# Row maxima taken chunk by chunk, a three-operand sum step, a 32-byte pad and a new list order in an attention and mixture-of-experts kernel

## The chip, the cores and the metric

The kernel runs on one core of a Trainium2 chip. The metric is the device time of one execution in microseconds; lower is better. Engine names are those of the profile: PE is the matrix engine (PEld its weight loads), DVE the vector engine, ACT the scalar engine, POOL is GpSimd, and SP issues most of the DMAs.

## What is computed

Attention first: 4 batches of 8 heads, 1152 keys of 64 numbers each, and 576 pooled queries (means of two neighbours). Then a mixture of 8 experts over the 2304 rows that result, with a gate that is normalised eight times by rows and by columns. All of it is float32.

```
q_pool = q.reshape(B, H, S // 2, 2, D).mean(axis=3)
scores = q_pool @ k.T / sqrt(D);  scores -= max(scores, axis=-1)
attn = exp(scores);  attn /= attn.sum(-1) + 1e-9;  x = attn @ v
P = exp(x @ w_gate - max);  8 times: P /= P.sum(1), P /= P.sum(0), P *= N / E
out = sum over e of P[:, e] * (relu(x @ w1[e]) @ w2[e])
```

## The kernel before

Attention works on 16 pairs of heads. A pair has five units: units 0 to 3 hold 128 queries of each of the two heads, and the fifth, mixed, holds the last 64 queries of both. For each unit PE makes scores S in three chunks of 384 keys (`qk`, L460; three products of split numbers for each head, 6 matmuls a chunk, 3 in a mixed one). DVE takes each chunk and head out of PSUM into the tile E and finds its row maximum on the way (`out_max`, L468). ACT then takes the exponential of a head's 1152 keys and its row sum (`expo`, L479). S has two buffers, so PE can be two chunks ahead of DVE.

The weights must stand keys-first for the product with V. There are two ways to get there. Units 2, 3 and the mixed one go through PE (`tr`, L506) and are copied out by ACT or DVE (`tr_out`, L516 and L518); then `av` (L535) multiplies. Units 0 and 1 are turned in blocks of 32 by DVE (`turn`, L489, into the tile `turned`), and 16 DMAs from SP's queue move the blocks to their places (`front`, L547, from `turned` into `fronted`); then `av_turned` (L556) multiplies both units at once. `turned` and `fronted` have one buffer each. So the DMAs of a pair can start only when its four turns are done and `av_turned` of the pair before has read `fronted`, and the next pair's turns can start only when these DMAs have landed.

Once in a pair `rec` (L581 to L584) adds 1e-9 to nine row sums on DVE, inverts them and turns them; the result goes through DRAM (`rd`, `RB`) and POOL multiplies x by it (L604). POOL also splits the next pair's queries and keys (`q_lo`, L416, and `k_lo`, L431).

The order of attention's instructions on all engines is made by a planner (`Plan.order`, L205): each step has a cost in ns, a due time and buffers, and the planner runs a list schedule over them. The due times come from `TR0`, `TD`, `UNIT`, `MIXED` and constants in the steps. Each engine then executes its list in order.

The experts follow in 96 steps. A step makes seven products of 6 matmuls each (`product`, L745 to L747; their tile in PSUM is psh, and they stream the split tokens `xch` and `xcl`), and 36 matmuls of the second layer (L785, tile pso, streaming `w2h` and `w2l`). The right-hand end of SBUF holds `turned` and `fronted` during attention, and `xch` and `xcl` after it in the same place.

Of the kernel before, what the change touches and what calls it, by code (L numbers as in the profile page):

```python
# [5 lines left out]
F32 = mybir.dt.float32  # L6
F32R = mybir.dt.float32r
ACTF = mybir.ActivationFunctionType
ALU = mybir.AluOpType
AX = mybir.AxisListType  # L10
PSUM = bass.MemoryType.PSUM
P = 128
# [19 lines left out]
def attention_moe(tc, q, k, v, w_gate, w1, w2, out):  # L32

    nc = tc.nc  # L40
    with (
        tc.tile_pool(name="const", bufs=1) as const,
        tc.tile_pool(name="stage", bufs=1, reuse_waits="tile") as stage,
    ):
        ident = const.tile([P, P], F32, name="ident")
        x = const.tile([P, ND, N], F32, name="x")
        wg = const.tile([P, ND, 32], F32, name="wg")
        PR = const.tile([P, NT, E], F32, name="PR")

        wt = Weights(nc, stage, w1, w2)  # L50
        blocks = Blocks(nc, stage, x)

        attention(tc, q, k, v, w_gate, x, ident, wg, PR, blocks, wt)
        moe(tc, out, x, ident, wg, PR, blocks, wt)
        blocks.pool.release()
# [250 lines left out]
            o["fn"](o["on"]) if isinstance(o["eng"], tuple) else o["fn"]()  # L306


TR0 = 14.0
TD = 22.0  # L310
STICK = 4.0
GAP = 145
GAP_R = 195
CAPS = dict(kr=2, qr=2, vt=2, kT=2, qT=2, S=2, tr=3, av=1, E=4, ET=2, st=4, rs=2, rt=2, RB=2, lg=1, T=1, F=1)
UNIT, MIXED = 4.4, 3.0
PAIR = QT * UNIT + MIXED
TURNED = 2

# [1 line left out]
def cost(eng, n, psum=False, two=False):  # L320
    if eng == "ACT":
        return n / 1.2 + (55 if psum else 93)
    if eng == "DVE":
        return n / (0.96 if psum or two else 1.92) + 69
    return (n * 2.3 + 150) if two else (n * 3.45 + 100)


def attention(tc, q, k, v, w_gate, xx, ident, wg, PR, blocks, wt, dry=False, NP=NPAIRS):
# [36 lines left out]
    def op(eng, cost, prio, r=(), w=(), new=(), use=(), lat=0, mode="", after=0):  # L365
        def put(fn):
            plan.op(eng, cost, prio, fn, r, w, new, use, lat, mode, after)
        return put
# [64 lines left out]
    def unit_ops(m):  # L433
# [12 lines left out]
        for j in range(NJ):  # L446

            @op("PE", 3 * 174, T + 1.2 * j, mode="T" if mixed else "R",
                r=[("kT", p, j if first else 0), ("qT", p, min(t, 1) if first else 0)], w=[("sc", m, j)],
                new=[(("sc", m, j), "S")] + ([(("E", m), "E"), (("st", m), "st")] if j == 0 else []),  # L450
                use=[("kT", p), ("qT", p)])
            def qk(j=j):
                if j == 0:
                    D["E", m] = sbt([P, 2, S], F32, "E")
                    D["st", m] = sbt([P, 2, 4], F32, "st")
                ps = D["sc", m, j] = pst([P, 2, 512], "S")
                for i, (x, y) in enumerate(prods):
                    for h in heads:
                        rows = slice(0, P) if mixed else slice(64 * h, 64 * h + 64)
                        nc.tensor.matmul(ps[:, h, :PK], D["qT", p][rows, x, t * P:(t + 1) * P],  # L460
                                         D["kT", p][rows, y, j * PK:(j + 1) * PK], start=(i == 0), stop=(i == 2))

            for h in heads:
                @op("DVE", cost("DVE", PK, True) + 20, T + 1.2 * j + 0.7 + 0.5 * h, r=[("sc", m, j)] + [("m3", m, h, j - 1)] * (j > 0), w=[("m3", m, h, j)],
                    use=[("sc", m, j), ("E", m), ("st", m)])
                def out_max(j=j, h=h):
                    st = D["st", m]
                    nc.vector.tensor_scalar(out=D["E", m][:, h, j * PK:(j + 1) * PK], in0=D["sc", m, j][:, h, :PK], scalar1=-0.0625,  # L468
                                            scalar2=st[:, h, j - 1:j] if j else None, op0=ALU.mult, op1=ALU.min, accum_out=st[:, h, j:j + 1])

        for h in heads:
            @op("ACT", S / 1.2 + 280, T + 4.4 + 1.3 * h, r=[("m3", m, h, NJ - 1)] + ([("X", m, 0)] if h else []), w=[("X", m, h)],
                new=[(("rs", p), "rs")] if t == 0 and h == 0 else [],
                use=[("st", m), ("E", m)] + ([("rs", p)] if h or t else []))
            def expo(h=h):
                if t == 0 and h == 0:
                    D["rs", p] = sums[p % caps["rs"]]
                x = D["E", m][:, h]
                nc.scalar.activation(out=x, in_=x, func=ACTF.Exp, bias=D["st", m][:, h, NJ - 1:NJ], scale=-1.0,  # L479
                                     accum_out=D["rs", p][:, col + h * QT:col + h * QT + 1])  # L480

        if turns:
            for h in heads:
                new = t == 0 and h == 0

                @op("DVE", cost("DVE", S, two=True) + 20, T + 5.8 + 1.3 * h, r=[("X", m, h)] + ([] if new else [("Y", p, 0, 0)]), w=[("Y", p, t, h)],
                    new=[(("T", p), "T")] if new else [], use=[("E", m)] + ([] if new else [("T", p)]))
                def turn(h=h):
                    nc.vector.transpose(turned[:, :, :, h, t].rearrange("p b c j -> p c b j"), D["E", m][:, h].rearrange("p (c b j) -> p c b j", b=4, j=BK))  # L489

            return
# [46 lines left out]
        if t == QT - 1 and p < NP - 1:  # L538
            @op("SP", 1, T - UNIT * (QT - 1) + 14, r=[("Y", p, i, h) for i in range(TURNED) for h in range(2)], w=[("F", p)], new=[(("F", p), "F")], use=[("T", p)])
            def room():  # L540
                pass

            for a in range(4):
                for z in range(4):
                    @op("SP", 600, T - UNIT * (QT - 1) + 14 + 0.6 * (4 * a + z), r=[("F", p)], w=[("Z", p, a, z)], use=[("T", p), ("F", p)], lat=2500)
                    def front(a=a, z=z):
                        nc.sync.dma_start(out=fronted[BK * z:BK * z + BK, a].rearrange("p c h t j -> p (c h t j)"),  # L547
                                          in_=turned[BK * a:BK * a + BK, z].rearrange("p c h t j -> p (c h t j)"))

            for j in range(3):  # L550
                @op("PE", 6 * 2 * 53.5 * TURNED, T - UNIT * (QT - 1) + TD + 0.7 * j, mode="C", r=[("v", p)] + [("Z", p, a, z) for a in range(4) for z in range(4)],
                    w=[("av", p, mixed)], use=[("v", p), ("F", p), ("av", p, mixed)])
                def av_turned(j=j):
                    for c in range(3 * j, 3 * j + 3):
                        for h in range(2):
                            nc.tensor.matmul(D["av", p, False][64 * h:64 * h + 64, :TURNED * P], D["v", p][:, h, c, :],  # L556
                                             fronted[:, :, c, h].rearrange("p a t j -> p a (t j)"), start=(c == 0), stop=(c == NC - 1))
                    if p == NP - 2 and j == 2:
                        low.release()
                        blocks.place(tc)  # L560

        if t == QT - 1 or mixed:
            n = w if mixed else QM
            F = T + TR0 + 4.8 if mixed or p == NP - 1 else T - UNIT * (QT - 1) + TD + 3
            o = b * Q + (QM if mixed else 0)

            @op("ACT", cost("ACT", n, True) + 100, F, r=[("av", p, mixed)], w=[("xu", p, mixed)], use=[("av", p, mixed)])
            def x_out():
                y, A, i = xx[:, hp, o:o + n], D["av", p, mixed], 0
                if not mixed and p < NP - 1:  # L570
                    i = TURNED * P
                    nc.scalar.activation(out=y[:, :i].rearrange("p (t a j) -> p a t j", a=4, j=BK),
                                         in_=A[:, :i].rearrange("p (a t j) -> p a t j", a=4, j=BK), func=ACTF.Copy)
                nc.scalar.activation(out=y[:, i:], in_=A[:, i:n], func=ACTF.Copy)

        if mixed:
            @op("DVE", 400, T + 8, r=[("X", p * (QT + 1) + i, h) for i in range(QT + 1) for h in (range(2) if i < QT else (0,))],
                w=[("r", p)], new=[(("rt", p), "rt")], use=[("rs", p)])
            def rec():
                y = D["rs", p][:, :2 * QT + 1]  # L580
                nc.vector.tensor_scalar(out=y, in0=y, scalar1=1e-9, scalar2=None, op0=ALU.add)  # L581
                nc.vector.reciprocal(y, y)
                D["rt", p] = sbt([P, BK], F32, "rt")
                nc.vector.transpose(D["rt", p], D["rs", p])  # L584
# [303 lines left out]
```

## Time and profile before

| what | value |
|---|---|
| time, median of 3 runs | 1978.65 us (1976.4 to 1979.98) |
| the profiled execution's own time | 1977.72 us |
| its span | 1975.9 us |
| PE busy | 1928.4 us, 98% |
| PE weight loads busy | 1695.2 us, 86% |
| DVE busy | 1479.0 us, 75% |
| ACT busy | 836.2 us, 42% |
| POOL busy | 434.1 us, 22% |
| first matmul of the experts | at 465.50 us |

A matmul's busy time overlaps that of the next one, so a busy PE may still wait: the distance from one start to the next says more. Attention is the first 465 us; its pairs of heads repeat, so one pair can be read for fifteen.

### The profile page before, as it was taken

The numbers are of one execution on the slowest core, as the hardware profiler recorded it, in microseconds if no ns is written. First come the engines' busy times: TensorE is split into PE (matmuls) and PEld (weight loads), VectorE is DVE, ScalarE is ACT, GpSimd is POOL, SyncE is SP. The second block draws the span as 40 slices with busy tenths as digits, with TensorE's granted clock in tenths as the row PEclk, the third lists the DMA queues.
The fourth block names the chain that finished last, engine by engine and source line by source line (L and its number), as shares of the span: only waits on it lengthen the run. The fifth ranks groups of instructions, "written<-read, shape, count | busy, mean of one in ns | idle before, by whom it ended". The sixth has DMA issues, their size and how long they took to land.

```text
span 1975.9 us, 30974 instructions
## 1 busy us (share of the span) xinstructions
PE 1928.4 (98%) x11957; PEld 1695.2 (86%) x11957; DVE 1479.0 (75%) x2885; ACT 836.2 (42%) x1434; POOL 434.1 (22%) x442
## 2 busy tenths in 40 slices
PE   7999999999999999999999999999999999999999
PEld 5777777678899999999899999999989999999997
DVE  7878887888987777767867776777787677777764
ACT  5766676665433333333343333333334333333331
POOL 3222232112012121222322122221222222121210
PEclk7999999999999999999999999999999999999999
DMA  7766666532131212212222221212222122222211
GB/s 227 184 145 159 162 178 160 136 89 65 60 107 54 75 65 65 79 61 75 85 75 65 65 76 64 75 63 66 65 91 85 60 75 65 65 67 72 75 46 41
DMA packets 63221, 177.02 MB, mean 90 GB/s; under 512 B 12768, under 2 KB 22624, under 8 KB 63072
## 3 DMA queue, kind: packets, MB, share of 16 engines
q1 hardware_dynamic: 62784, 174.63, 30.2%
q8 instruction: 94, 1.54, 0.3%
q14 instruction: 55, 0.45, 0.1%
q10 hardware_dynamic: 288, 0.39, 0.1%
HBM read 134.81 MB, written 4.79 MB: 71 GB/s over the span
## 4 chain that ended last, share of the span: by engine, by line
PE 72%; DVE 3%; DMA 1%; ACT 0%; issue 0%; POOL 0%; SPq 0%; DVEq 0%; ACTq 0%
PE pso L785 37%; PE psh L747 12%; PE psh L745 12%; PE psh L746 11%; DVE w1l L147 1%; DMA w2s<-in_moe_w_dram 1%; DVE w2l L158 0%; DVE xcl L98 0%; DVE x L795 0%; DVE c L765 0%; DVE hl L755 0%; ACT w2h L157 0%; ACT hh L754 0%; POOL ca L729 0%; ACT w1h L142 0%
## 5 line engine op out<-in xcount | busy, mean ns | idle before, releaser
L745 PE MATMUL psh<-xch,w1h 128*128 128x384 f32 x1344 | 456.4, 340 | 3.1 <-ACT p L760 1.7
L746 PE MATMUL psh<-xcl,w1h 128*128 128x384 f32 x1344 | 455.5, 339 | 0.0
L747 PE MATMUL psh<-xch,w1l 128*128 128x384 f32 x1344 | 454.7, 339 | 0.7 <-DVE w1l L147 0.7
L785 PE MATMUL pso<-w2h,hh 128*128 128x512 f32 x1152 | 448.7, 389 | 0.0
L785 PE MATMUL pso<-w2l,hh 128*128 128x512 f32 x1152 | 448.7, 389 | 0.0
L785 PE MATMUL pso<-w2h,hl 128*128 128x512 f32 x1152 | 448.4, 389 | 0.0
L754 ACT ACTIVATE hh<-c 128x384 fp32r<-128x384 f32 x384 | 200.1, 522 | 289.8 <-DVE c L765 289.5
L795 DVE SCALAR_TENSOR_TENSOR x<-pso,PR,x 128x512 f32<-128x512 f32 x264 | 196.9, 746 | 152.7 <-PE pso L785 152.5
L128 POOL TENSOR_TENSOR w1t<-w1s 128x256 f32<-128x256 f32 x88 | 67.9, 771 | 1037.6 <-DMA w1s<-in_moe_w_dram 855.8
L745 PEld LDWEIGHTS psh<-xch,w1h 128*128 128x128 f32 x1344 | 252.8, 188 | 9.3 <-ACT p L760 2.4
L746 PEld LDWEIGHTS psh<-xcl,w1h 128*128 128x128 f32 x1344 | 252.7, 188 | 3.5
L785 PEld LDWEIGHTS pso<-w2h,hl 128*128 128x128 f32 x1152 | 216.2, 188 | 45.2
L747 PEld LDWEIGHTS psh<-xch,w1l 128*128 128x128 f32 x1344 | 252.6, 188 | 1.8 <-DVE w1l L147 1.6
L785 PEld LDWEIGHTS pso<-w2h,hh 128*128 128x128 f32 x1152 | 216.3, 188 | 42.1 <-ACT hh L754 0.5
L785 PEld LDWEIGHTS pso<-w2l,hh 128*128 128x128 f32 x1152 | 216.2, 188 | 41.6
L157 ACT ACTIVATE w2h<-w2s 128x1024 fp32r<-128x1024 f32 x96 | 101.9, 1061 | 274.4 <-PE pso L785 182.3
L755 DVE SCALAR_TENSOR_TENSOR hl<-c,hh 128x384 fp32r<-128x384 f32 x384 | 211.0, 550 | 3.0 <-ACT hh L754 2.2
L460 PE MATMUL S<-kT,qT 64*128 64x384 f32 (+1 forms) x1296 | 179.4, 371 | 32.4 <-DVE E L468 28.9
L479 ACT ACTIVATE E<-E,st 128x1152 f32<-128x1152 f32 x144 | 179.8, 1250 | 69.0 <-DVE E L468 68.9
L468 DVE TENSOR_SCALAR_CACHE_REDUCE E<-S,st 128x384 f32<-128x384 f32 x288 | 163.9, 606 | 50.3 <-PE S L460 48.5
L158 DVE TENSOR_TENSOR w2l<-w2s,w2h 128x1024 fp32r<-128x1024 f32 x96 | 133.3, 1388 | 84.6 <-ACT w2h L157 84.6
L760 ACT ACTIVATE p<-psh 128x384 f32<-128x384 f32 x96 | 47.1, 490 | 332.9 <-PE psh L747 332.5
(90 smaller groups left out, 2268.4 us busy)
## 6 DMA issues: line engine op xcount, KB each, us to landing
w1s<-in_moe_w_dram SPq DMA_DIRECT2D x96, 512.0 KB
w2s<-in_moe_w_dram SPq DMA_DIRECT2D x96, 512.0 KB
fronted<-turned SPq DMA_DIRECT2D x240, 144.0 KB
qr<-in_q_dram SPq DMA_DIRECT2D x15, 640.0 KB
vt<-in_v_dram SPq DMA_DIRECT2D x16, 576.0 KB
kr<-in_k_dram SPq DMA_DIRECT2D x15, 576.0 KB
out_dram<-x SPq DMA_DIRECT2D x18, 256.0 KB
RB<-rd SPq DMA_DIRECT2D x32, 128.0 KB
```

Source lines behind the costliest of these rows:

```text
L157: self.nc.scalar.activation(out=hi, in_=self.raw2[k], func=ACTF.Copy)
L158: self.nc.vector.tensor_tensor(out=lo, in0=self.raw2[k], in1=hi.bitcast(F32), op=ALU.subtract)
L460: nc.tensor.matmul(ps[:, h, :PK], D["qT", p][rows, x, t * P:(t + 1) * P], D["kT", p][rows, y, j * PK:(j + 1) * PK], start=(i == 0), stop=( ...
L468: nc.vector.tensor_scalar(out=D["E", m][:, h, j * PK:(j + 1) * PK], in0=D["sc", m, j][:, h, :PK], scalar1=-0.0625, scalar2=st[:, h, j - 1: ...
L479: nc.scalar.activation(out=x, in_=x, func=ACTF.Exp, bias=D["st", m][:, h, NJ - 1:NJ], scale=-1.0, accum_out=D["rs", p][:, col + h * QT:col ...
L745: nc.tensor.matmul(ps, hi[:, a, c, :], blocks.xch[:, b, c, :], start=(c == 0), stop=False)
L746: nc.tensor.matmul(ps, hi[:, a, c, :], blocks.xcl[:, b, c, :], start=False, stop=False)
L747: nc.tensor.matmul(ps, lo[:, a, c, :], blocks.xch[:, b, c, :], start=False, stop=(c == 1))
L754: nc.scalar.activation(out=hh[:, fh, ts], in_=src, func=ACTF.Relu)
L755: nc.vector.scalar_tensor_tensor(out=hl[:, fh, ts], in0=src, scalar=0.0, in1=hh[:, fh, ts].bitcast(F32), op0=ALU.max, op1=ALU.subtract)
L785: nc.tensor.matmul(ps, u[:, fh, ms], w[:, fh, :], start=(n == 0), stop=(n == 11))
L795: nc.vector.scalar_tensor_tensor(out=a, in0=ps, scalar=PR[:, m, e:e + 1], in1=a, op0=ALU.mult, op1=ALU.add)
```

## The change

Five things are changed.

1. `out_max` no longer passes a chunk's maximum on as the starting value of the next. It writes the scaled score with its sign kept and leaves one maximum for each chunk in `st`; a new step `neg`, one TENSOR_REDUCE on DVE in each unit, joins the three and negates. `expo` waits for `neg`.
2. `rec` adds 1e-9 by a SCALAR_TENSOR_TENSOR whose second tensor is the same tile, in place of a TENSOR_SCALAR.
3. A tile of 32 bytes is put at the right-hand end of SBUF before everything else there. It moves `turned`, `fronted`, `xch` and `xcl` down by 32 bytes and no other tile.
4. The planner's numbers are others: `TR0` and `TD`, `UNIT` and `MIXED`, the costs of three DVE steps and of the `front` DMAs, and a lag behind `x_out`.
5. By these numbers and the new step, the planner makes another order.

```
+        tc.tile_pool(name="edge", bufs=1, side="right") as edge,
...
+        edge.tile([P, 8], F32, name="edge")
...
-TR0 = 14.0
-TD = 22.0
+TR0 = 10.0
+TD = 30.0
...
-UNIT, MIXED = 4.4, 3.0
+UNIT, MIXED = 4.0, 1.8
...
-                @op("DVE", cost("DVE", PK, True) + 20, T + 1.2 * j + 0.7 + 0.5 * h, r=[("sc", m, j)] + [("m3", m, h, j - 1)] * (j > 0), w=[("m3", m, h, j)],
+                @op("DVE", 480, T + 1.2 * j + 0.7 + 0.5 * h, r=[("sc", m, j)], w=[("m3", m, h, j)],
...
-                    nc.vector.tensor_scalar(out=D["E", m][:, h, j * PK:(j + 1) * PK], in0=D["sc", m, j][:, h, :PK], scalar1=-0.0625,
-                                            scalar2=st[:, h, j - 1:j] if j else None, op0=ALU.mult, op1=ALU.min, accum_out=st[:, h, j:j + 1])
+                    nc.vector.tensor_scalar(out=D["E", m][:, h, j * PK:(j + 1) * PK], in0=D["sc", m, j][:, h, :PK], scalar1=0.0625,
+                                            scalar2=None, op0=ALU.mult, op1=ALU.max, accum_out=st[:, h, j:j + 1])
+
+        @op("DVE", 80, T + 4.1, r=[("m3", m, h, j) for j in range(NJ) for h in heads], w=[("m", m)], use=[("st", m)])
+        def neg():
+            st = D["st", m]
+            nc.vector.tensor_reduce(out=st[:, :nt, 3:4], in_=st[:, :nt, 0:3], axis=AX.X, op=ALU.max, negate=True)
...
-                nc.scalar.activation(out=x, in_=x, func=ACTF.Exp, bias=D["st", m][:, h, NJ - 1:NJ], scale=-1.0,
+                nc.scalar.activation(out=x, in_=x, func=ACTF.Exp, bias=D["st", m][:, h, 3:4],
...
-                    @op("SP", 600, T - UNIT * (QT - 1) + 14 + 0.6 * (4 * a + z), r=[("F", p)], w=[("Z", p, a, z)], use=[("T", p), ("F", p)], lat=2500)
+                    @op("SP", 720, T - UNIT * (QT - 1) + 14 + 0.6 * (4 * a + z), r=[("F", p)], w=[("Z", p, a, z)], use=[("T", p), ("F", p)], lat=2500)
...
-                nc.vector.tensor_scalar(out=y, in0=y, scalar1=1e-9, scalar2=None, op0=ALU.add)
+                nc.vector.scalar_tensor_tensor(out=y, in0=y, scalar=1e-9, in1=y, op0=ALU.add, op1=ALU.max)
```

What the new order is shows best at three places that come back in every pair. The first is PE around `av_turned`. In the names, av is the product with V, ET the copied-out transposes, and S the chunks of scores. Before:

```order
L460 MATMUL S_1177<-kT_725,qT_715 128x384 x6
L460 MATMUL S_1186<-kT_725,qT_715 128x384 x6
L535 MATMUL av_1088<-ET_1040,vt_613 64x128 x18
L556 MATMUL av_1088<-fronted_79,vt_613 64x256 x18
L460 MATMUL S_1237<-kT_725,qT_715 128x384 x6
L460 MATMUL S_1249<-kT_725,qT_715 128x384 x6
L535 MATMUL av_1258<-ET_1153,vt_613 64x64 x18
L460 MATMUL S_1283<-kT_725,qT_715 128x384 x6
```

Now, at the same place of a pair:

```order
L462 MATMUL S_1167<-kT_754,qT_707 128x384 x6
L513 MATMUL tr_1179<-ident_65,E_993 128x128 x4
L513 MATMUL tr_1185<-ident_65,E_993 128x128
L542 MATMUL av_1091<-ET_1047,vt_619 64x128 x18
L462 MATMUL S_1217<-kT_754,qT_707 128x384 x6
L462 MATMUL S_1225<-kT_754,qT_707 128x384 x6
L563 MATMUL av_1091<-fronted_83,vt_619 64x256 x18
L462 MATMUL S_1258<-kT_754,qT_707 128x384 x6
L462 MATMUL S_1270<-kT_754,qT_707 128x384 x6
L542 MATMUL av_1279<-ET_1160,vt_619 64x64 x18
```

Two chunks of scores now stand between `av` and `av_turned`, which stood back to back. (The trace counts 36 instructions where a row of av here has 18.)

The second place is DVE around `rec` and a pair's first turns (STREAM_TRANSPOSE into `turned`). Before:

```order
L468 TENSOR_SCALAR E_2040,st_2041<-S_2053,st_2041 128x384 x2
L581 TENSOR_SCALAR rs1_77<-rs1_77 128x9
L582 RECIPROCAL rs1_77<-rs1_77 128x9
L584 STREAM_TRANSPOSE rt_2094<-rs1_77 128x32
L468 TENSOR_SCALAR E_2040,st_2041<-S_2080,st_2041 128x384 x2
L468 TENSOR_SCALAR E_2096,st_2097<-S_2098 128x384 x2
L489 STREAM_TRANSPOSE turned_78<-E_2040 128x9x4x32
L468 TENSOR_SCALAR E_2096,st_2097<-S_2137,st_2097 128x384 x2
L489 STREAM_TRANSPOSE turned_78<-E_2040 128x9x4x32
L468 TENSOR_SCALAR E_2096,st_2097<-S_2147,st_2097 128x384 x2
L518 COPY ET_2176<-tr_2188 128x512
L468 TENSOR_SCALAR E_2198,st_2199<-S_2200 128x384 x2
```

Now:

```order
L470 TENSOR_SCALAR E_1719,st_1720<-S_1774 128x384 x2
L476 TENSOR_REDUCE st_1720<-st_1720 128x2
L588 SCALAR_TENSOR_TENSOR rs0_80<-rs0_80 128x9
L589 RECIPROCAL rs0_80<-rs0_80 128x9
L591 STREAM_TRANSPOSE rt_1815<-rs0_80 128x32
L470 TENSOR_SCALAR E_1818,st_1819<-S_1820 128x384 x2
L496 STREAM_TRANSPOSE turned_82<-E_1719 128x9x4x32
L470 TENSOR_SCALAR E_1818,st_1819<-S_1832 128x384 x2
L496 STREAM_TRANSPOSE turned_82<-E_1719 128x9x4x32
L470 TENSOR_SCALAR E_1818,st_1819<-S_1859 128x384 x2
L476 TENSOR_REDUCE st_1819<-st_1819 128x2
L470 TENSOR_SCALAR E_1907,st_1908<-S_1909 128x384 x2
```

`rec` has moved behind the last chunk of unit 0, and the copy between the turns has gone elsewhere.

The third place is SP's queue after the moves into `fronted`. Before:

```order
L547 DMA fronted_79<-turned_78 32x1152 x4
L396 DMA vt_1631<-in_v_dram 128x1152
L547 DMA fronted_79<-turned_78 32x1152 x12
L590 DMA rd_1765<-rt_1753 9x32 x4
L383 DMA qr_1803<-in_q_dram 128x1280
```

Now:

```order
L554 DMA fronted_83<-turned_82 32x1152 x3
L398 DMA vt_1657<-in_v_dram 128x1152
L554 DMA fronted_83<-turned_82 32x1152 x13
L385 DMA qr_1811<-in_q_dram 128x1280
L597 DMA rd_1827<-rt_1815 9x32 x4
```

The load of the next queries now stands right behind the sixteen moves, ahead of what waits for `rec`.

## Rows read from the trace of the kernel before

**Rows 1.** Two pairs by stretch: busy us (instructions) of each engine, PEclk, DMA share, GB/s.

```profile
281.50:308.00 26.50, 25.44 (x274) 19.68 (x272) 23.20 (x67) 18.52 (x34) 7.35 (x5) 1.00 0.63 160
308.00:340.00 32.00, 27.87 (x272) 21.96 (x274) 23.07 (x65) 18.39 (x34) 7.22 (x5) 0.89 0.58 149
```

**Rows 2.** DVE's first and sixteenth RECIPROCAL: start, duration, line, operation, tiles, count.

```profile
37.52 0.22 DVE L582 RECIPROCAL rs<-rs 128x9 f32<-128x9 f32 x1
...
451.15 0.22 DVE L582 RECIPROCAL rs<-rs 128x9 f32<-128x9 f32 x1
```

**Rows 3.** DVE's groups, 50 to 440 us: count, busy us, mean ns, idle before.

```profile
L468 DVE TENSOR_SCALAR_CACHE_REDUCE E<-S,st 128x384 f32<-128x384 f32 x256 | 145.6, 606 | 48.5 <-PE S L460 46.8
L489 DVE STREAM_TRANSPOSE turned<-E 128x1152 f32<-128x1152 f32 x52 | 71.3, 1373 | 18.4 <-DMA rd<-rt 6.6 <-DMA fronted<-turned 5.6 <-ACT ET L516 3.5
L468 DVE TENSOR_SCALAR_CACHE_REDUCE E<-S 128x384 f32<-128x384 f32 x128 | 66.3, 551 | 2.6 <-PE S L460 2.4
...
L581 DVE TENSOR_SCALAR rs<-rs 128x9 f32<-128x9 f32 x14 | 19.2, 1370 | 0.0
```

**Rows 4.** DVE in order of time in one pair, idle time before in brackets.

```profile
281.53 1.46 DVE L581 TENSOR_SCALAR rs<-rs 128x9 f32<-128x9 f32 x1
...
285.83 1.38 DVE L489 STREAM_TRANSPOSE turned<-E 128x1152 f32<-128x1152 f32 x1 [0.34 <-ACT E L479]
...
294.40 1.38 DVE L489 STREAM_TRANSPOSE turned<-E 128x1152 f32<-128x1152 f32 x1
298.21 0.62 DVE L468 TENSOR_SCALAR_CACHE_REDUCE E<-S,st 128x384 f32<-128x384 f32 x1 [2.43 <-PE S L460]
...
307.82 1.45 DVE L581 TENSOR_SCALAR rs<-rs 128x9 f32<-128x9 f32 x1
```

**Rows 5.** PE in order of time in the same pair, around av_turned.

```profile
291.38 2.19 PE L535 MATMUL av<-ET,vt 128*64 128x128 f32 x36
293.39 4.05 PE L556 MATMUL av<-fronted,vt 128*64 128x256 f32 x36
297.38 1.32 PE L460 MATMUL S<-kT,qT 64*128 64x384 f32 x12
```

**Rows 6.** SP's issues in the same pair, in order of time.

```profile
297.49 3.60 SPq L547 DMA_DIRECT2D fronted<-turned  x4
...
301.76 7.91 SPq L547 DMA_DIRECT2D fronted<-turned  x12
```

**Rows 7.** DVE in order of time: a turn that waits, a rec without POOL beside it.

```profile
259.55 1.38 DVE L489 STREAM_TRANSPOSE turned<-E 128x1152 f32<-128x1152 f32 x1 [0.78 <-DMA rd<-rt]
...
424.42 0.17 DVE L581 TENSOR_SCALAR rs<-rs 128x9 f32<-128x9 f32 x1
```

**Rows 8.** POOL in order of time in the pair of rows 4.

```profile
281.40 1.56 POOL L416 TENSOR_TENSOR qT<-qr,qT 128x640 fp32r<-128x640 f32 x1 [4.61 <-ACT qT L411]
282.92 2.66 POOL L431 TENSOR_TENSOR kT<-kr,kT 128x1152 fp32r<-128x1152 f32 x1
```

**Rows 9.** The nearest TENSOR_REDUCE, among the groups of the whole trace.

```profile
L721 DVE TENSOR_REDUCE rs<-PR 128x18 f32<-128x144 f32 x8 | 2.4, 294 | 0.0
```

**Rows 10.** The chain that ended last, 584 to 617 us: start, duration, what.

```profile
584.81 8.17 PE pso L785 x36
...
600.41 8.17 PE pso L785 x36
```

**Rows 11.** PE in the experts' first step; sixteen starts lie from one to the other.

```profile
467.14 0.33 PE L747 MATMUL psh<-xch,w1l 128*128 128x384 f32 x1
...
469.91 0.33 PE L746 MATMUL psh<-xcl,w1h 128*128 128x384 f32 x1
```

**Rows 12.** A group of two-tensor DVE instructions, then one of them, then POOL beside it.

```profile
L147 DVE TENSOR_TENSOR w1l<-w1s,w1h 128x256 fp32r<-128x256 f32 x96 | 43.2, 450 | 0.0
...
950.15 1.41 DVE L147 TENSOR_TENSOR w1l<-w1s,w1h 128x256 fp32r<-128x256 f32 x1
...
949.12 2.16 POOL L91 TENSOR_TENSOR xt<-x,xt 128x768 f32<-128x768 f32 x1 [10.36 <-DVE xcl L98]
```

More of the change, by code (lines that the diff above doesn't have):

```diff
@@ L467, in out_max @@
                     st = D["st", m]
-                    nc.vector.tensor_scalar(out=D["E", m][:, h, j * PK:(j + 1) * PK], in0=D["sc", m, j][:, h, :PK], scalar1=-0.0625,
-                                            scalar2=st[:, h, j - 1:j] if j else None, op0=ALU.mult, op1=ALU.min, accum_out=st[:, h, j:j + 1])
+                    nc.vector.tensor_scalar(out=D["E", m][:, h, j * PK:(j + 1) * PK], in0=D["sc", m, j][:, h, :PK], scalar1=0.0625,
[4 more added lines that the diff above has]
+            nc.vector.tensor_reduce(out=st[:, :nt, 3:4], in_=st[:, :nt, 0:3], axis=AX.X, op=ALU.max, negate=True)
         for h in heads:
-            @op("ACT", S / 1.2 + 280, T + 4.4 + 1.3 * h, r=[("m3", m, h, NJ - 1)] + ([("X", m, 0)] if h else []), w=[("X", m, h)],
+            @op("ACT", S / 1.2 + 280, T + 4.4 + 1.3 * h, r=[("m", m)] + ([("X", m, 0)] if h else []), w=[("X", m, h)],
                 new=[(("rs", p), "rs")] if t == 0 and h == 0 else [],
@@ L484, in unit_ops @@
                 new = t == 0 and h == 0
-                @op("DVE", cost("DVE", S, two=True) + 20, T + 5.8 + 1.3 * h, r=[("X", m, h)] + ([] if new else [("Y", p, 0, 0)]), w=[("Y", p, t, h)],
+                @op("DVE", 1300, T + 5.8 + 1.3 * h, r=[("X", m, h)] + ([] if new else [("Y", p, 0, 0)]), w=[("Y", p, t, h)],
                     new=[(("T", p), "T")] if new else [], use=[("E", m)] + ([] if new else [("T", p)]))
@@ L565, in unit_ops @@
             o = b * Q + (QM if mixed else 0)
-            @op("ACT", cost("ACT", n, True) + 100, F, r=[("av", p, mixed)], w=[("xu", p, mixed)], use=[("av", p, mixed)])
+            @op("ACT", cost("ACT", n, True) + 100, F, r=[("av", p, mixed)], w=[("xu", p, mixed)], use=[("av", p, mixed)], lat=0 if p == NP - 1 else 5000)
             def x_out():
```

## The prediction

> **What bounds the kernel now.** I read the stages first, then one pair of attention engine by engine, then one step of the experts.
>
> The experts are bound by PE. In the chain that ended last, a block of 36 pso matmuls starts at 584.81 and the next at 600.41, 15.60 us apart [rows 10]. The 36 take 8.17 us (0.227 each), so the 42 psh matmuls of a step take the other 7.43 us, 0.1769 us each, and no gap is left. Only cheaper matmuls can shorten this stage.
>
> Attention is bound by a ring through the two single buffers `turned` and `fronted`. From the first RECIPROCAL to the sixteenth there are 15 periods in 413.63 us, 27.58 us each [rows 2]. A calm one runs from 281.53 to 307.82, 26.29 us [rows 4], and in that stretch DVE is busy 23.2 of 26.5 us, so no engine fills it [rows 1]. Follow the ring: the first turn starts at 285.83, the fourth at 294.40 and ends at 295.78, 9.95 us later [rows 4]. PE runs av and av_turned back to back from 291.38 to 297.44 [rows 5], 1.66 us beyond the last turn. The first move into `fronted` is issued at 297.49, right behind, and the sixteenth ends its issue at 309.67, 12.18 us later [rows 6]. What is left of 26.29 us, 26.29 - 11.66 - 12.18 = 2.45 us, passes until the next pair's first turn; that is the landing. That landing bounds the turns is seen at 259.55, where DVE waits 0.78 us for a DMA [rows 7]. The long PE stretch has a second price: DVE runs dry and waits 2.43 us for scores at 298.21 [rows 4].
>
> **The change part by part.**
>
> *Order.* Two chunks of scores now stand between av and av_turned. This block of PE starts 1.24 us before what follows it (297.38 to 298.62 in the trace, 1.32 with its tail [rows 5]), and DVE gets its first chunk 0.83 us after the block's start (297.38 to 298.21 [rows 4, 5]). Take the block's start as zero. av_turned ends at 1.24 + 4.05 = 5.3. DVE, by the new list, does three maxima, a turn, a maximum and the last turn: 0.83 + 4 x 0.48 + 2 x 1.37 = 5.5 (0.551 and 1.373 are the groups' durations [rows 3]; 0.48 is my estimate for the distance of starts, which is shorter than a duration because neighbours overlap). So av_turned no longer ends 1.66 us after the last turn but with it. From first turn to last, one copy is gone and one reduction has come, and six maxima lose 0.055 us: 9.95 becomes about 9.5. The ring is then 9.5 + 12.2 + landing. Most pairs have a longer landing than the calm one. One pair ran at a lower granted clock (308 to 340: 0.89, 32.0 against 26.5 us [rows 1]); without its extra 5.5 us the mean period is (413.6 - 5.5) / 15 = 27.2 us and its landing 27.2 - 11.66 - 12.18 = 3.4. The new ring is 9.5 + 12.2 + 3.4 = 25.1 us. The price of the lost cover: DVE's wait of 2.43 falls to about 0.6, because it has scores while av runs.
>
> *Maxima.* The chained form takes 606 ns, the unchained 551 [rows 3]; 18 of 27 in a pair change: -1.0 us of DVE a pair. Against it stand five reductions of six numbers. None is in the trace. From below, a nine-element DVE instruction takes 0.17 us [rows 7]; from above, the nearest TENSOR_REDUCE, of 144 numbers, takes 0.294 [rows 9]. I take 0.2, nearer to the small one: +1.0 us. The two cancel, within -0.2 to +0.5. `expo` now also waits for the other head, 0.5 us later; behind it the turns wait for DMAs anyway, and if that cover goes, it costs that 0.5 us a pair.
>
> *rec.* The TENSOR_SCALAR on nine numbers takes 1.46 us at 281.53 [rows 4] and 0.17 us at 424.42 [rows 7]; fourteen take 19.2 us [rows 3]. At 281.53 POOL's L416 had begun at 281.40 and ends at 282.96, when rec ends too; beyond POOL nothing differs [rows 8]. So 1.29 us a pair are a wait behind POOL. Does the new form, with two tensors from SBUF, wait too? Two-tensor instructions do: a w1l of 256 columns, 0.45 in the mean, takes 1.41 us at 950.15 and ends 0.28 us after a POOL instruction that began a microsecond earlier [rows 12]. Moreover rec now comes later, behind unit 0's last chunk, where by the lists POOL is at L431, which takes 2.66 us [rows 8]. Bounds: -1.29 us (no wait), or +1.2 us (2.66 in place of 1.46) a pair on DVE. It stands just ahead of the first turns.
>
> The Trainium skill, "SBUF — State Buffer", section "Who interferes with whom", says that a DVE instruction with two SBUF inputs contends with a GpSimd instruction that reads SBUF, and that the single-source form does so in its two-port modes. By it the edit buys nothing whenever POOL is first, and rec keeps a wait; the trace agrees for tensor pairs.
>
> *Both together.* DVE's work in a pair, 23.2 us [rows 1], becomes 23.2 - 1.0 + 1.0 - 1.3 = 21.9 without the wait and 24.4 with it; about twelve small copies moved from ACT to DVE in all add under 0.5 a pair. With the wait, and 0.6 us dry before av_turned's scores, DVE sets 24.4 + 0.5 + 0.6 = 25.5; without it the ring sets 25.1. I take 25.5, since the rows show the waiting case. 27.2 - 25.5 = 1.7 us by 15 periods: **-25 us**. The ends: 24.2 (landing as in the calm pair, 2.45 us, and no wait), -45 us; and 26.4 (wait and a dearer reduction added to the ring's 25.1), -12 us. The dip of the clock I leave as it is (-5.5 us if it goes). The first pair and the end of attention have the same matmuls in another order; I take 0, and -3 to +3.
>
> *The pad.* It moves xch and xcl, the streams of all psh matmuls, by 32 bytes, and `turned` and `fronted` with them. Does the place matter? In steady steps a psh starts every 176.9 ns [rows 10]; but in the first step sixteen start in 2.77 us, 173.1 ns each [rows 11]. By pso's 0.227 us for 512 columns and 173.1 for 384, a column costs 0.42 ns, one cycle at the higher level of the clock, 2.4 GHz; so the first step fits pso, whose stream does not move, and a steady psh carries 3.8 ns too much. If the place is the reason, the pad takes it from 42 x 96 = 4032 matmuls: 15 us, less the few already quick, **-14 us**. If not: 0. If the new place is the worse one, +14 by the same figure. That the same place gave both speeds speaks against; that pso shows no such surplus speaks for. I take -14, with little over even odds. The moves by DMA through the shifted tiles are 12.2 us of the ring; I take no change.
>
> **Sum.** The profiled execution took 1977.72 us (span 1975.9 and 1.8 around it), 0.93 below the median of the runs. -25 - 14 gives 1938.7 for it, **1940** against the median.
>
> **Rivals.**
>
> *The pad does nothing* (the change there does not do what it might): 1978.65 - 25 = 1954. For: rows 11; against: pso.
>
> *The ring doesn't get shorter, because its DMAs are the slow part.* DMA share in a calm pair is 0.63 [rows 1], most of it while the sixteen moves run, and the next queries' load now follows directly behind them. If the landing grows from 3.4 to 5 us, the ring is 26.7 and attention gains 0.5 x 15 = 7 us: 1971 without the pad's gain, 1957 with it. Against: the load stands behind the moves in the same queue.
>
> *Slower: PE runs dry and the granted clock falls.* The pair at 308 had a mean of 0.89 in place of 1.00 (1 is 2.4 GHz, the lower level is 1.2) and took 5.5 us more [rows 1]. If rec's longer wait delays the turns and PE stands still in many pairs, each costs 5.5 us. Five more such pairs eat attention's 25 us, seven the whole 39; from there on the kernel is slower. With ten, and nothing from the pad, it is 1954 + 55 = 2009. Against: the new order spreads PE's work, and the calm pair, in which DVE ran dry once for 2.43 us, held 1.00 [rows 1, 4].
>
> **How the numbers follow.** Both gains, 1940: 0.43 (own range 1930 to 1950). Pad nothing, 1954: 0.32. The DMA rival, 1957 to 1976: 0.13. Slower: 0.06. More than forecast, below 1924, with dips gone and the calm landing: 0.06. The range 1924 to 1966 leaves out the last two and half of the DMA rival. A change of 0.2%, 4 us, is what a measurement of this kernel can tell from none. Faster by more: 0.88; within: 0.06, from the DMA rival's upper end; slower: 0.06.
>
> **What would show it.** A pair's period near 25.5 in place of 26.3 to 27; PE's av and av_turned apart, the first move issued as the fourth turn ends, DVE's wait for scores after av_turned under 1 us; rec's first instruction at 0.2 us (no wait) or at 1 to 2.6 us beside L431 of POOL (wait); maxima of 551 ns only; psh at 173 ns and a step of 15.45 us (pad), or still 15.60. The forecast is wrong if the period stays above 26.5, or if stretches of lower clock become more.

## The result and the profile after

Five runs of the changed kernel took 1949.3 us in the median (1945.41 to 1950.06), five of the kernel before on the same chip 1976.4 (1972.43 to 1979.98). The ratio is 0.9856, with a 95% interval of 0.9838 to 0.9875: faster by some 28 us. The forecast was 1940, the range 1924 to 1966. The profiled execution took 1945.41 us with a span of 1943.5, against 1975.9 before. The first matmul of the experts starts at 442.71 instead of 465.50, so attention gave 22.8 us and all behind it 9.6. This execution was the fastest of the five: its span is 32.4 us shorter, where the medians differ by 27.

Two stretches of attention by engine: busy us (instructions) of PE, PEld, DVE, ACT and POOL, granted clock, DMA share, GB/s. They answer to [rows 1].

```profile
173.54:199.28 25.74, 24.69 (x272) 19.71 (x272) 22.49 (x71) 17.97 (x33) 7.25 (x4) 1.00 0.68 174
...
308.00:340.00 32.00, 30.75 (x352) 24.20 (x349) 29.15 (x87) 20.71 (x38) 7.74 (x5) 1.00 0.64 158
```

A pair takes 25.74 us here. The stretch from 308 to 340, which held a dip of the clock to 0.89 before, now stands at 1.00 throughout. After the first 30 us one dip is left, at a place where the kernel before has one too; first the kernel before, then the kernel after:

```profile
120.00:130.00 10.00, 6.49 (x51) 4.88 (x51) 7.74 (x17) 5.92 (x13) 1.55 (x1) 0.87 0.52 158
```

```profile
120.00:130.00 10.00, 8.33 (x78) 5.64 (x76) 9.07 (x21) 3.13 (x6) 1.55 (x1) 0.83 0.22 82
```

DVE's first and sixteenth RECIPROCAL, in order of time, against [rows 2]:

```profile
40.07 0.22 DVE L589 RECIPROCAL rs<-rs 128x9 f32<-128x9 f32 x1
...
432.78 0.22 DVE L589 RECIPROCAL rs<-rs 128x9 f32<-128x9 f32 x1
```

Fifteen periods are 392.71 us, 26.18 each (27.58 before). The last of them is 29.92 us, longer than before (26.53), since the end of attention is ordered differently; the first fourteen are 25.9 each against 27.7.

DVE's groups from 50 to 440 us: count, busy us, mean ns, idle time before them and what ended it. They answer to [rows 3].

```profile
L470 DVE TENSOR_SCALAR_CACHE_REDUCE E<-S 128x384 f32<-128x384 f32 x389 | 197.6, 549 | 32.3 <-PE S L462 31.7
L496 DVE STREAM_TRANSPOSE turned<-E 128x1152 f32<-128x1152 f32 x53 | 72.9, 1375 | 9.5 <-ACT ET L523 4.3 <-DMA fronted<-turned 2.5 <-DMA qr<-in_q_dram 1.7
...
L588 DVE SCALAR_TENSOR_TENSOR rs<-rs 128x9 f32<-128x9 f32 x15 | 16.0, 1068 | 0.8 <-ACT E L486 0.8
L476 DVE TENSOR_REDUCE st<-st 128x2 f32<-128x6 f32 x58 | 9.3, 161 | 2.0
```

The maxima are all of the 549 ns form, and the idle time ahead of them fell from 51.1 us (48.5 and 2.6) to 32.3. The joining reduction takes 161 ns. The addition's mean of 1068 ns mixes two kinds, as shown further down.

One pair in order of time, first DVE, then PE, then SP's issues; they answer to [rows 4 to 6].

```profile
173.54 1.38 DVE L496 STREAM_TRANSPOSE turned<-E 128x1152 f32<-128x1152 f32 x1 [1.40 <-ACT ET L523]
...
181.44 1.37 DVE L496 STREAM_TRANSPOSE turned<-E 128x1152 f32<-128x1152 f32 x1
183.72 0.56 DVE L470 TENSOR_SCALAR_CACHE_REDUCE E<-S 128x384 f32<-128x384 f32 x1 [0.91 <-PE S L462]
```

```profile
174.17 2.19 PE L542 MATMUL av<-ET,vt 128*64 128x128 f32 x36
176.28 0.80 PE L462 MATMUL S<-kT,qT 64*128 64x384 f32 x6
178.13 0.79 PE L462 MATMUL S<-kT,qT 64*128 64x384 f32 x6 [1.05 <-DVE E L470]
178.85 4.11 PE L563 MATMUL av<-fronted,vt 128*64 128x256 f32 x36
```

```profile
183.00 1.80 SPq L554 DMA_DIRECT2D fronted<-turned  x3
...
185.85 10.32 SPq L554 DMA_DIRECT2D fronted<-turned  x13
```

`av_turned` (L563) now stands behind two chunks of scores, between which PE waits 1.05 us for a score buffer, and ends at 182.96; the fourth turn ends at 182.81, and the first move is issued at 183.00. DVE's wait for scores behind the last turn is 0.91 us instead of 2.43.

Two blocks of pso, three steps of the experts apart, from the chain that ended last (start, duration, what), against [rows 10]:

```profile
577.19 8.20 PE pso L792 x36
...
623.71 8.20 PE pso L792 x36
```

The step is 15.51 us instead of 15.60; the 36 pso take 8.20 instead of 8.17, and the 42 psh 7.31 instead of 7.43, 174.0 ns each.

### The profile page after: what moved, and what is told of

It is laid out like the page before. It is cut to its first block, busy times and chain, and to the rows that moved or that the text cites. A ratio compares the mean times of both kernels' runs of the same rounds, so it can differ in the third digit from the quotient of the medians.

```text
span 1943.5 us, 30922 instructions
## 1 busy us (share of the span) xinstructions
PE 1910.2 (98%) x11957; PEld 1681.8 (87%) x11957; DVE 1482.4 (76%) x2976; ACT 832.1 (43%) x1423; POOL 432.3 (22%) x442
## 4 chain that ended last, share of the span: by engine, by line
PE 84%; DVE 8%; DMA 4%; SPq 2%; ACT 1%; issue 1%; POOL 0%; DVEq 0%; ACTq 0%
PE pso L792 39%; PE psh L754 12%; PE psh L752 12%; PE psh L753 12%; PE S L462 4%; PE av L563 3%; DVE E L470 2%; SPq L554 2%; DVE turned L496 2%; PE tr L513 2%; PE av L542 2%; DMA fronted<-turned 1%; DMA vt<-in_v_dram 1%; DVE rs L588 1%; DVE w1l L149 0%
## 5 line engine op out<-in xcount | busy, mean ns | idle before, releaser
L752 PE MATMUL psh<-xch,w1h 128*128 128x384 f32 x1344 | 451.1, 336 | 2.9 <-ACT p L767 1.5
L754 PE MATMUL psh<-xch,w1l 128*128 128x384 f32 x1344 | 449.6, 336 | 0.6 <-DVE w1l L149 0.6
L753 PE MATMUL psh<-xcl,w1h 128*128 128x384 f32 x1344 | 450.1, 335 | 0.0
L470 DVE TENSOR_SCALAR_CACHE_REDUCE E<-S 128x384 f32<-128x384 f32 x432 | 219.6, 549 | 34.6 <-PE S L462 33.8
```

What stands on the lines that cost most here:

```text
L752: nc.tensor.matmul(ps, hi[:, a, c, :], blocks.xch[:, b, c, :], start=(c == 0), stop=False)
L753: nc.tensor.matmul(ps, hi[:, a, c, :], blocks.xcl[:, b, c, :], start=False, stop=False)
L754: nc.tensor.matmul(ps, lo[:, a, c, :], blocks.xch[:, b, c, :], start=False, stop=(c == 1))
```

## The experiments

Each kernel was run in turn with the kernel before on one chip, whose medians went from 1976 to 1981 us from one chip to the next. So ratios are compared; 0.001 of one is 2 us. "First matmul" is that of the experts in the profiled execution: where attention ends.

### Which part shortens attention

**Numbers alone** (the kernel before with all of the planner's new numbers; the new costs of the maxima, the turns and the moves and the lag behind `x_out` are left out here):

```
-TR0 = 14.0
-TD = 22.0
+TR0 = 10.0
+TD = 30.0
-UNIT, MIXED = 4.4, 3.0
+UNIT, MIXED = 4.0, 1.8
...
```

> The kernel before with the planner's new numbers and costs alone (old chained maxima, old addition, no pad). If the new order of the list gives attention's gain: mean period about 26 us in place of 27.6, about 1956 us. Rival (the gain comes from DVE's work: split maxima and the other addition): period above 27, about 1973 to 1977 us.

Measured: 2010.27 us, ratio 1.0151 [1.0131, 1.0171], slower by 30 us; first matmul at 491.39. Both expectations fall. One pair of it, DVE, then PE, in order of time, then two stretches by engine (columns as above):

```profile
212.06 2.24 DVE L581 TENSOR_SCALAR rs<-rs 128x9 f32<-128x9 f32 x1
...
216.44 1.38 DVE L489 STREAM_TRANSPOSE turned<-E 128x1152 f32<-128x1152 f32 x1 [1.65 <-DMA rd<-rt]
```

```profile
213.67 2.11 PE L506 MATMUL tr<-ident,E 128*128 128x128 f32 x15
218.81 0.80 PE L460 MATMUL S<-kT,qT 64*128 64x384 f32 x6 [3.03 <-DVE E L468]
```

```profile
211.00:221.00 10.00, 6.66 (x71) 5.18 (x69) 8.29 (x19) 5.10 (x10) 4.81 (x3) 0.99 0.75 213
221.00:231.00 10.00, 10.00 (x97) 7.70 (x93) 7.38 (x20) 4.01 (x7) 0.00 (x0) 0.84 0.07 16
```

In this list the first turn follows `rec` directly. `rec` takes 2.24 us, the turn then waits 1.65 us for the moves to land, and the maxima that would free a score buffer stand behind it: PE has nothing to do for 3.03 us, and in the next ten the granted clock is 0.84 (1 is 2.4 GHz). Read in stretches of 10 us, a lower clock (0.74 to 0.96) comes in twelve of the sixteen pairs. It is the slower rival's mechanism, except that it took the new numbers alone to bring it out. How much of the 30 us this stall makes up is not shown; no run took it away by itself.

**Split maxima alone** (old numbers, old addition, no pad):

```
-@op("DVE", cost("DVE", PK, True) + 20, ..., r=[("sc", m, j)] + [("m3", m, h, j - 1)] * (j > 0), ...)
+@op("DVE", 480, ..., r=[("sc", m, j)], ...)
+@op("DVE", 80, T + 4.1, r=[... all six maxima ...], w=[("m", m)], ...)  # neg
-scalar2=st[:, h, j - 1:j] if j else None, op0=ALU.mult, op1=ALU.min
+scalar2=None, op0=ALU.mult, op1=ALU.max
...
```

> The kernel before with maxima per chunk and the joining reduction alone (old numbers, old addition, no pad). By the durations: 18 maxima a pair lose 0.055 us, 1.0 us of DVE, and five reductions of 0.16 us come, 0.8: -0.2 us a pair and exponentials that wait for both heads. If that is all: 1974 to 1980 us. Rival (the chain itself held the turns up): period 26.5 us, about 1962 us.

Measured: 1953.1 us, ratio 0.9878 [0.9864, 0.9891]; first matmul at 441.98, and no dip of the clock in attention after its first 30 us. The period is 26.04 us in each of twelve pairs. So this part alone is worth the whole of attention's gain, and the expectation by durations fails. But the edit does two things: it changes the instructions, and through its costs and its new step it changes the list.

**The same list with the old instructions** (that kernel, but the chained maxima are issued, `neg` issues nothing, and `expo` reads the chain's last value again, which is left out here):

```
-scalar1=0.0625, scalar2=None, op0=ALU.mult, op1=ALU.max
+scalar1=-0.0625, scalar2=st[:, h, j - 1:j] if j else None, op0=ALU.mult, op1=ALU.min
 def neg():
-    nc.vector.tensor_reduce(...)
+    pass
...
```

> The list of work of the run with split maxima on the old numbers (so the planner counts 480 ns for each maximum, sees no chain and books a slot for the joining reduction), but the old chained maxima are issued in it and the joining reduction issues nothing. If the place of the instructions in the list made that run's gain of 24 us: period 26.0 to 26.3 us, 1950 to 1957 us, though each chained maximum again takes 60 ns more from start to start. Rival (the cheaper, unchained instructions made it): period 27.5 us, about 1977 us.

Measured: 1945.07 us, ratio 0.9824 [0.9809, 0.9839]; first matmul at 435.50. The list makes the gain; the instructions are not needed for it and cost a little. Its pair by engine, DVE's turns from 50 to 440 us, then DVE and PE in order of time:

```profile
165.19:190.63 25.44, 24.57 (x276) 19.75 (x272) 22.48 (x64) 18.45 (x34) 7.17 (x5) 1.00 0.69 181
```

```profile
L493 DVE STREAM_TRANSPOSE turned<-E 128x1152 f32<-128x1152 f32 x52 | 70.0, 1365 | 11.4 <-ACT E L483 11.4
```

```profile
164.34 0.82 DVE L585 TENSOR_SCALAR rs<-rs 128x9 f32<-128x9 f32 x1
...
168.18 1.38 DVE L493 STREAM_TRANSPOSE turned<-E 128x1152 f32<-128x1152 f32 x1
...
173.83 2.64 DVE L493 STREAM_TRANSPOSE turned<-E 128x1152 f32<-128x1152 f32 x2 [0.88 <-ACT E L483]
```

```profile
170.70 2.19 PE L539 MATMUL av<-ET,vt 128*64 128x128 f32 x36
172.72 4.05 PE L560 MATMUL av<-fronted,vt 128*64 128x256 f32 x36
```

Between `rec` and the first turn stand four maxima, as before; but between the first turn and the fourth there are four instead of eight, and no copy, so the fourth ends 8.29 us after the first begins instead of 9.95. The turn at 168.18 does not wait: the moves land under DVE's work. All that the turns still wait for is an exponential (0.88 us ahead of the third), while before they waited 18.4 us, much of it for DMAs [rows 3]. `av` and `av_turned` are back to back as before, but `av_turned` starts 4.54 us behind the first turn (172.72 - 168.18) instead of 7.56 [rows 4, 5], and ends at 176.77, 0.3 us behind the last turn's end instead of 1.66. The ring is shorter than the work around it. What sets the 25.44 us now is not shown: PE is the fullest engine with 24.57 of them, but it was the fullest before too (25.44 of 26.50 [rows 1]).

**The list of the kernel after with the old instructions** (the same replacement in the kernel after):

> The list of the kernel after, with the old chained maxima issued in it and no joining reduction. If the list counts: the maxima cost 18 x 60 ns more a pair and the reductions 5 x 0.2 less, nothing in sum, 1949 us within 4. Rival (the new planner numbers need the unchained maxima, and the chain is why the numbers alone gave 2010 us): 1975 to 2010 us, with a dip of the clock in most pairs.

Measured: 1953.84 us, ratio 0.9868 [0.9853, 0.9883], which can't be told from the kernel after. So there, too, the list counts and not the form of the maxima. The rival falls: the chain is not why the numbers alone are slow. Here `rec` waits in 15 of 16 pairs and still costs the kernel little (DVE's group from 50 to 440 us, columns as above):

```profile
L587 DVE SCALAR_TENSOR_TENSOR rs<-rs 128x9 f32<-128x9 f32 x15 | 35.7, 2377 | 0.8 <-ACT E L485 0.8
```

### What the addition's form does

The rows of the kernel after show a race: POOL's `k_lo` (L433), then `rec`, in a pair in which it waits and in one in which it does not.

```profile
63.38 2.66 POOL L433 TENSOR_TENSOR kT<-kr,kT 128x1152 fp32r<-128x1152 f32 x1 [1.69 <-ACT kT L428]
...
63.40 2.66 DVE L588 SCALAR_TENSOR_TENSOR rs<-rs 128x9 f32<-128x9 f32 x1
...
195.53 2.72 POOL L433 TENSOR_TENSOR kT<-kr,kT 128x1152 fp32r<-128x1152 f32 x1 [1.70 <-ACT kT L428]
...
195.56 0.16 DVE L588 SCALAR_TENSOR_TENSOR rs<-rs 128x9 f32<-128x9 f32 x1
```

**The one-tensor form** in the kernel after:

```
-nc.vector.scalar_tensor_tensor(out=y, in0=y, scalar=1e-9, in1=y, op0=ALU.add, op1=ALU.max)
+nc.vector.tensor_scalar(out=y, in0=y, scalar1=1e-9, scalar2=None, op0=ALU.add)
```

> The kernel after with the addition to the row sums as the one-tensor instruction of before. The three-operand form took 0.16 us in nine pairs and 2.2 to 2.7 us in six, those in which POOL's k_lo began first by more than 23 ns. If only the start order decides and the form nothing: the same split, 1949 us within 3. If the one-tensor form waits behind POOL more readily (it holds a second port): it waits in nearly all pairs, 2.6 us each, up to 9 more pairs, 1951 to 1965 us. If the one-tensor form doesn't wait behind this k_lo: 0.17 us in all, 1940 to 1949 us.

Measured: 1947.05 us, ratio 0.9853 [0.9835, 0.9872], the same as the kernel after. It took 161 to 165 ns in twelve pairs and 2.2 to 2.7 us in three, 1.3 in the last. Between these two forms nothing is decided by the form, only by the order of starts.

**The accumulating form**, whose extra result goes to a spare column:

```
+spare = sb.tile([P, 1], F32, name="spare")
...
-nc.vector.scalar_tensor_tensor(out=y, in0=y, scalar=1e-9, in1=y, op0=ALU.add, op1=ALU.max)
+nc.vector.tensor_scalar(out=y, in0=y, scalar1=1e-9, scalar2=None, op0=ALU.add, op1=ALU.max, accum_out=spare)
```

> The kernel after with the addition as a one-tensor instruction that also accumulates a maximum into a spare column (as the maxima do). If that form does not wait for POOL: at most 0.25 us in every pair, six waits of 2.5 us gone; where they stood on the ring up to 15 us less, and where PE's or the transfers' waits take their place nothing: 1936 to 1949 us, I expect 1943. Rival (it waits as the three-operand form does): the same split, 1949 us.

Measured: 1946.64 us, ratio 0.9847 [0.9834, 0.9861]. The wait is gone in all sixteen pairs, at most 165 ns, also where `k_lo` had begun 37 ns before, as here (POOL, then DVE):

```profile
113.92 2.67 POOL L434 TENSOR_TENSOR kT<-kr,kT 128x1152 fp32r<-128x1152 f32 x1 [1.69 <-ACT kT L429]
...
113.96 0.16 DVE L589 TENSOR_SCALAR_CACHE_REDUCE rs<-rs 128x9 f32<-128x9 f32 x1
```

The ratio falls by 0.0009, within the intervals. In the kernel after, the six waits of 2.5 us are hidden, at least in part: without them the turns wait longer, 15.4 us in the same window instead of 9.5.

```profile
L497 DVE STREAM_TRANSPOSE turned<-E 128x1152 f32<-128x1152 f32 x53 | 72.9, 1376 | 15.4 <-ACT ET L524 8.3 <-DMA rd<-rt 3.3 <-DMA qr<-in_q_dram 1.8
```

### What the pad does

**The pad alone**, of 32 bytes, on the kernel before:

```
+tc.tile_pool(name="edge", bufs=1, side="right") as edge,
+edge.tile([P, 8], F32, name="edge")
```

> The kernel before with the 32-byte pad and nothing else. If the place of the streams of the experts' first matmuls sets their pace: psh starts every 174.0 ns in place of 176.8, 4032 of them, 11 us, less what pso gives back (0.8 ns each in 3456, 2.7 us): a step of 15.50 us and about 1968 us in all; attention's mean period unchanged near 27.5 us. Rival (the pace follows from what the new order leaves in TensorE's queue at the end of attention, not from the place): step 15.60, about 1977 us.

Measured: 1969.07 us, ratio 0.9957 [0.9942, 0.9973], as expected from the place.

**The kernel after without it** (the same two lines removed):

> The kernel after without the pad. If the place counts and nothing else of the experts' gain comes from the order: step back to 15.60 us, psh 176.8 ns, about 1949 + 9 = 1958 us, attention unchanged (first expert matmul near 443). Rival (the pad does nothing): 1949 us, step 15.50.

Measured: 1954.44 us, ratio 0.9881 [0.9865, 0.9897]: some 5 us slower than the kernel after, with intervals that overlap, but the step tells it plainly.

**64 bytes** (`[P, 16]`) and **128 bytes** (`[P, 32]`) on the kernel before:

> The kernel before with a pad of 64 bytes, so that the tiles below it move but stand to a 64-byte boundary as they did before. If only the rest on 64 counts: step 15.60 us, about 1977 us. If any move of the streams off their old place helps (a conflict with another tile's place): step 15.50, about 1968 us.

> The kernel before with a pad of 128 bytes. If the place modulo 128 bytes is what makes the old place slow: step 15.59 us again, psh 176.7 ns. If any move off the old place helps, or the distance to another tile counts: 15.45 to 15.51 us.

Measured: 64 bytes gave 1963.82 us, ratio 0.993 [0.9916, 0.9945]; 128 bytes, in one execution, 1966.49 beside 1973.3 of the kernel before. Two blocks of pso of each, three steps apart, from the chain that ended last; first the kernel after without the pad, then 32, 64 and 128 bytes on the kernel before:

```profile
579.22 8.17 PE pso L790 x36
...
626.00 8.17 PE pso L790 x36
```

```profile
574.76 8.20 PE pso L787 x36
...
621.28 8.20 PE pso L787 x36
```

```profile
582.92 8.16 PE pso L787 x36
...
629.26 8.16 PE pso L787 x36
```

```profile
582.93 8.20 PE pso L787 x36
...
629.39 8.20 PE pso L787 x36
```

The steps are 15.59, 15.51, 15.45 and 15.49 us. Less the pso and divided by 42, a psh starts every 176.7, 174.0, 173.5 and 173.5 ns. So the place decides between 176.7 and 174.0 ns, with the old order and with the new. Rest on a 64-byte boundary is not what counts (64 bytes more leave it as it was), nor is the place modulo 128. Every move off the old place helped; what the old place collides with stays open.

### Versions that beat both

**The kernel after with the accumulating addition and 64 bytes** (both edits above):

> The kernel after with the accumulating addition and a pad of 64 bytes in place of 32. Attention as with the accumulating addition alone (first expert matmul near 438 us); experts as with the 64-byte pad on the kernel before: step 15.45 in place of 15.51 us, 5.5 us less over the stage. 1941 us. Rival (the 64-byte pad's faster step hangs on the old order): 1946.5 us.

Measured: 1936.17 us, ratio 0.9782 [0.9763, 0.9801].

**The kernel with split maxima alone, the accumulating addition and 64 bytes**, old planner numbers:

> The kernel before with split maxima, the accumulating addition and a pad of 64 bytes; old planner numbers. Split maxima alone gave 1953 us with a period of 26.04 us in every calm pair and an addition that took 1.19 us. If the addition is on what sets the period: 1.0 us less in 13 pairs, and 11.6 us less in the experts by the step of 15.45: 1928 us. If PE sets the period: 1941 us. A rival that is worse: TensorE waits differently and the clock dips come back, 5 us each.

Measured: 1932.46 us, ratio 0.9762 [0.9747, 0.9777], the fastest; first matmul at 435.08. Its period is 25.44 us against 26.04 without the new addition: of the 1.03 us that the addition lost (1.19 to 0.16), 0.6 reached the end. Here, unlike in the kernel after, the addition's wait is on the path, since the first turn behind it hardly waits (some 0.2 us). (The pad came with it; alone on the kernel before it left attention's mean period at 27.5 us.) The period is the same 25.44 us as in the list with the old maxima, where the addition took 0.82 us: something else ends both there, and what it is stays open. The list with the old maxima, this addition and this pad together were not tried.

## Why the prediction was right, and where it was not

*What bounds attention.* Right for the kernel before. The ring through `turned` and `fronted` was the bound, and where it got shorter than the other work (the list with the old instructions), no turn waits for the DMAs any longer. "No engine fills it" passed over PE, which was busy 25.44 of 26.5 us [rows 1]; the shortest steady period in these runs is 25.44 us.

*Order, and attention's -25 us.* The steps happened as written: from the first turn to the end of the fourth 9.28 us (median of twelve pairs, 9.5 forecast, 9.95 before), from there to the first move 0.18 (0 forecast, 1.70 before), DVE's wait behind the turns 0.91 (0.6 forecast, 2.43 before). The last turn and `av_turned` both ended some 6.6 us behind the start of the two chunks, not 5.3 to 5.5, since PE waited between the chunks; but they ended together, which is what counted. Three things were off. First, the 25.5 us a pair was DVE's sum with a wait of `rec` in every pair, and that was the wrong path: `rec` waited in six of fourteen. Second, the ring did not come to 25.1. The way from the first move to the next pair's first turn, taken as 12.2 + 3.4 = 15.6 us, measured 16.6 (median of thirteen pairs; 15.8 before), and also 16.5 in the kernel with the accumulating addition, where no `rec` waits; with the 9.46 us ahead of it that makes 26.0, and the fourteen pairs took 25.9 each. Third, of the 22.8 us some 5.5 are the dip between 308 and 340, which the forecast left in place: the ring alone gave about 17. So that attention came within 2.2 us of the forecast is in part luck. What the forecast did not separate is who makes the list. It described one order made by the numbers and the new step together; the runs show that the numbers alone cost 30 us, the new entry of the maxima alone gains 24, or 35 with the old instructions. Such parts do not add up.

*Maxima and reductions cancel.* Right in the kernel after: old and new instructions in its list can't be told apart (0.9868 and 0.9856). The reduction was taken as 0.2 us and has 0.161. In the shorter list of the old numbers the new instructions came out 0.0054 behind; some 0.4 of the 0.6 us a pair between them are a longer wait of `rec` (1.19 instead of 0.82). The rest was not separated; with the accumulating addition the new instructions, too, reach 25.44 us.

*rec.* The bounds were right (0.16 to 2.66 us), but neither end holds for every pair: which one comes is decided anew in each. In the kernel after and in that with the one-tensor form the two start within 50 ns of each other in most pairs; where POOL's record begins 17 to 23 ns before DVE's, DVE is through in 0.16 us (with an exception at 22, and one at 19 in the list with the old maxima), and from 24 ns on it waits for POOL's end. It waited in six of the first fourteen. The Trainium skill, "SBUF — State Buffer", section "Who interferes with whom", says that the order of issue decides who blocks, and that a tensor-scalar form that also writes its accumulator is not among those that take the ports shared with GpSimd. The runs here agree: the one-tensor form waits like the three-operand form (2.65 us), and the accumulating form never (0.15 to 0.165). The cost put on the wait, 25.5 instead of 25.1 us a pair or 6 us in all, is not borne out: taking the waits away was worth 1.8 us in all by the ratios, which their intervals can't tell from nothing.

*The pad, -14 us.* The mechanism was right, the size was not. The step fell by 0.09 us, not 0.15: psh went to 174.0 ns and not to 173.1, which saves 4032 x 2.8 = 11 us, and pso, whose streams were not moved, went from 227.0 to 227.8 ns (8.17 and 8.20 us for 36), which gives back 3456 x 0.8 = 2.7. The 64-byte pad, with 173.5 and no slower pso, gave 0.007 of the ratio, the 14 us of the forecast.

*Sum.* The forecast for the profiled execution was 1938.7; it took 1945.41. Of the 6.7 us between them attention's share is 2.2 (22.8 instead of 25) and that of the part behind it 4.4 (9.6 instead of 14). By the medians the miss is larger, 27 us gained of the 39 forecast.

*Rivals.* That the pad does nothing: fell by the runs with and without it on both lists. That the landing grows: not the landing itself, which from the end of the last move's issue to the next turn is 4.1 us and read in the same way 4.6 before; but the whole way from the first move to the next turn grew by 0.8 (issuing the moves took 12.3 us in the median instead of 11.7). Slower through the granted clock: it happened in the kernel with the numbers alone; in the kernel after one dip is left (0.83 from 120 to 130), beside a like one before, and that of 308 to 340 is gone.

## What to carry to other kernels

A scheduler's cost entry can be worth more than the instruction that it describes: run the new list with the old instructions before crediting the instruction. Judge a wait by what stands behind it: the same addition was worth 0.6 us a pair in a list where the turn came in time, and nothing that the intervals can tell from zero where the turn waited for a DMA. Where a matmul stream starts a few ns late in steady state, move its tile by several small offsets and read the distance of starts, not the durations.

## What the runs showed of the hardware that was not expected

- A DVE addition on nine numbers beside POOL's `k_lo` takes 0.16 us where POOL's record begins up to 23 ns ahead of its own (two exceptions, at 22 and 19 ns) and 2.65 us where it is 24 to 40 ns ahead; the form that also accumulates took at most 0.165 us in all sixteen pairs.
- Where POOL's record began first and DVE did not wait, POOL's `k_lo` was only some 0.05 us longer (2.70 to 2.72 instead of 2.65 to 2.67).
- The place of a psh stream in SBUF sets its pace: 176.7 ns at the old place, 174.0, 173.5 and 173.5 at 32, 64 and 128 bytes below it; pso's own pace moved by 0.8 ns with 32 and 128 bytes, though its streams stood still.
